# Interleaving the last block's tokens in PSUM, storing them over all 128 partitions, and joining two projection bursts

## The chip, the cores and the metric

One core of one Trainium2 chip runs the whole kernel. The number that counts is the device time of one execution in microseconds (us). Shares of time below are shares of the profiled execution, whose span from first to last instruction is 306.2 us.

The engines are named as in the profile: PE is TensorE (its weight loads are PEld), DVE is VectorE, ACT is ScalarE, POOL is GpSimd, SP is SyncE. A queue that only issues DMAs is written SPq, ACTq or POOLq.

## What is computed

A kernelised attention feeds a two-layer perceptron. Shapes: 8 batches, 8 heads, 576 tokens, head dimension 64, 128 random features; the perceptron takes 4608 tokens of 512 and has 2048 hidden units.

```python
def _attn_ref(q, k, v, omega):
    # q, k scaled by D ** -0.25
    def phi(x):
        h = x @ omega.T - sum(x * x) / 2
        return exp(h - max(h)) / sqrt(m)
    q_p, k_p = phi(q), phi(k)
    kv = einsum('bhsm,bhsd->bhmd', k_p, v);  z = sum(k_p, axis=2)
    return (q_p @ kv) / (q_p @ z + 1e-6)          # [8, 8, 576, 64]

def _moe_ref(x, w_in, w_out):                      # x: [4608, 512], the heads side by side
    h = x @ w_in                                   # [4608, 2048]
    g = h * clip(h + 3, 0, 6) / 6
    return g @ w_out                               # [4608, 512]
```

576 tokens are not a multiple of 128. The kernel takes 512 tokens of each batch as that batch's own block (blocks 0 to 7) and gathers the 64 left over from each of the 8 batches into a ninth block of 512 (block 8). Column `64 * b + s` of that block is left-over token `s` of batch `b`; with `b = 2 * t + a` it is column `(t a s)`, t slowest.

## The kernel before

The program is a list of operations with their dependencies. A table `ORDER` gives each engine its sequence, which was found by a search outside the kernel. PSUM is one ring of eight banks; an operation claims the banks that it needs at its place in PE's sequence and they come free when their last reader is done.

**Projections of queries and keys, batches 3 to 7.** Two 64-row matmuls run side by side in the array's two halves of rows. Each entry of `BURSTS` is one such burst over a range of token columns. The small range `(0, 2)` holds the left-over rows and takes two banks; each of the others takes four.

```python
TU = [(0, 2), (2, 6), (6, 10), (10, 14), (14, 18)]
BURSTS = [[(0, 2)], [(2, 6)], [(6, 10)], [(10, 14)], [(14, 18)]]
...
def burst(n, ranges):
    parts = [(d0, d1, [Virt(ring, True) for _ in range(2 if d1 - d0 == 2 else 4)]) for d0, d1 in ranges]
    ...
    def e(E):
        for part in parts:
            d0, d1, _ = part
            for x in range(d1 - d0):
                for lh in range(2):
                    E.matmul(out_of(part, 0, lh)[0][:, 128 * x:128 * x + 128], kT[64 * lh:64 * lh + 64, d0 + x, :],
                             om[64 * lh:64 * lh + 64, lh, :], start=x == 0, stop=True, skip_group_check=True)   # L766
            for lh in range(2):
                ins = E.matmul(out_of(part, 1, lh)[0], om[64 * lh:64 * lh + 64, lh, :],
                               qT[64 * lh:64 * lh + 64, d0:d1, :], start=d1 - d0 == 4, stop=True,
                               skip_group_check=True)                                                           # L769
        return ins
    # then four exponentials on ACT for each range empty its banks
```

**First layer of blocks 7 and 8.** A seven-product scheme (Strassen's, in Winograd's form) over 2 x 2 blocks. One product is two accumulating matmuls of 256 columns into half a PSUM bank:

```python
def two(E, dst, w, x, start=False):
    for c in range(2):
        ins = E.matmul(dst, w(c), x[:, c, :], start=start and c == 0, stop=c == 1, skip_group_check=True)   # L1126
    return ins

def e_a(E):
    two(E, half(U, 0), orig(0, 0), b[0][0], True)
    return two(E, half(U, 1), summed(W3s), X3s[u])
def e_b(E):
    two(E, half(V, 1), summed(W2s), X2s[u])
    return two(E, half(U, 0), orig(0, 1), b[1][0])
# mm1c: one more two() into half(V, 0)
def e_d(E):
    two(E, half(V, 1), orig(1, 1), X4s[u])
    return two(E, half(V, 0), summed(W4s), b[1][1])
```

These run for `f` = 0 to 7 in each of the two blocks. ACT and DVE move seeds and sums between the halves, apply the activation, and write `gT` (hidden units on partitions, tokens along the row) in the column order that PSUM has.

**Second layer and stores of block 8.** `gT[:, f, 128 * j:128 * j + 128]` is the stationary operand, so 128 consecutive token columns become the 128 output partitions. With columns `(t a s)` partitions 0 to 63 are batch `2t` and 64 to 127 are batch `2t + 1`, so each store is cut into two of 64 partitions.

```python
def last_product():
    for n, (j, e0, e1) in enumerate(((0, 0, 256), (1, 0, 128), (1, 128, 256))):
        ...  # eight matmuls (L1371), one DVE addition (L1379), then
        for x in range(2):
            ... E.dma_start(ends[x, MAIN:S, j, 256 + e0:256 + e1], osb[64 * x:64 * x + 64, j, 256 + e0:256 + e1])   # L1383

def store(blk, i, c0, c1, t):
    ...
    else:                                           # block 8
        x = out.rearrange("(t a s) e -> a s t e", a=2, s=S)
        parts = [(64 * a, 64, x[a, MAIN:S, 2 * i:2 * i + 2, c0:c1]) for a in range(2)]
    for p0, n, dst in parts:
        ... E.dma_start(dst, osb[p0:p0 + n, 2 * i:2 * i + 2, c0:c1])                                                # L1400
```

Block 8 has three calls of `store` (six DMAs) and three pieces in `last_product` (six more): twelve DMAs, spread over SPq and ACTq.

Of the kernel before, what the change touches and what calls it, by code (L numbers as in the profile page):

```python
# [20 lines left out]
        118, 13, 124, 139, 144, 156, 115, 150, 168, 147, 153, 133, 127, 121, 142, 162, 165, 183, 171, 159, 175, 177,  # L21
        136, 185, 212, 130, 173, 197, 214, 179, 219, 254, 199, 187, 181, 242, 227, 189, 204, 202, 257, 229, 244, 217,
        222, 403, 404, 232, 234, 415, 247, 416, 417, 409, 410, 249, 411, 405, 406, 412, 418, 207, 421, 424, 252, 237,
        260, 280, 427, 430, 433, 300, 436, 288, 284, 282, 439, 286, 442, 306, 303, 445, 290, 315, 324, 309, 448, 451,
        312, 292, 294, 454, 296, 318, 457, 298, 333, 321, 583, 584, 331, 573, 337, 574, 335, 575, 339, 585, 586, 587,
        327, 341, 588, 576, 353, 345, 589, 343, 577, 329, 355, 366, 578, 579, 593, 368, 379, 371, 594, 595, 358, 392,
        590, 384, 381, 394, 397, 580, 374, 596, 597, 598, 361, 387, 603, 400, 599, 600, 621, 627, 624, 639, 636, 604,
        630, 642, 645, 505, 651, 492, 660, 501, 654, 495, 657, 486, 605, 507, 511, 606, 503, 607, 474, 509, 666, 483,
        498, 477, 480, 672, 608, 669, 513, 489, 609, 792, 610, 675, 519, 782, 515, 517, 527, 783, 539, 798, 541, 544,
        532, 551, 785, 529, 786, 563, 793, 556, 565, 568, 553, 695, 795, 796, 702, 799, 801, 802, 723, 805, 806, 709,  # L30
        736, 809, 815, 716, 824, 812, 818, 830, 741, 827, 839, 833, 842, 748, 854, 848, 845, 750, 860, 738, 760, 857,
        772, 753, 863, 765, 970, 774, 777, 971, 762, 980, 973, 974, 981, 883, 986, 983, 984, 890, 987, 989, 990, 897,
        1003, 1000, 1012, 997, 993, 994, 1006, 911, 1015, 924, 1021, 1027, 929, 1018, 936, 1033, 1030, 904, 926, 1048,
        1042, 1036, 941, 938, 1045, 960, 1051, 1174, 1158, 1159, 965, 948, 962, 1168, 953, 950, 1161, 1071, 1169,
        1162, 1078, 1171, 1172, 1175, 1085, 1177, 1178, 1191, 1092, 1185, 1188, 1194, 1200, 1215, 1203, 1112, 1206,
        1209, 1218, 1181, 1182, 1124, 1117, 1224, 1221, 1230, 1236, 1114, 1099, 1239, 1233, 1126, 1136, 1346, 1347,
        1129, 1141, 1138, 1356, 1148, 1349, 1150, 1153, 1350, 1357, 1259, 1287, 1359, 1360, 1266, 1362, 1365, 1366,
        1273, 1363, 1379, 1376, 1373, 1382, 1388, 1300, 1394, 1369, 1302, 1312, 1391, 1305, 1314, 1397, 1370, 1317,
        1406, 1336, 1409, 1418, 1338, 1403, 1421, 1412, 1280, 1424, 1427, 1550, 1341, 1534, 1535, 1544, 1454, 1537,
        1545, 1447, 1324, 1538, 1326, 1329, 1547, 1548, 1461, 1551, 1553, 1468, 1557, 1554, 1488, 1475, 1490, 1558,  # L40
        1500, 1493, 1561, 1502, 1505, 1512, 1579, 1517, 1514, 1567, 1582, 1524, 1570, 1526, 1600, 1529, 1591, 1564,
        1615, 1609, 1594, 1576, 1606, 1585, 1612, 1660, 1673, 1597, 1663, 1629, 1665, 1676, 1702, 1630, 1668, 1678,
        1689, 1632, 1633, 1692, 1639, 1694, 1705, 1681, 1718, 1707, 1640, 1697, 1731, 1721, 1642, 1723, 1643, 1734,
        1710, 1747, 1736, 1648, 1649, 1760, 1726, 1750, 1739, 1807, 1645, 1763, 1752, 1646, 1765, 1820, 1755, 1810,
        1652, 1812, 1653, 1836, 1768, 1823, 1776, 1825, 1815, 1777, 1839, 1849, 1828, 1841, 1779, 1852, 1865, 1844,
        1854, 1780, 1878, 1868, 1786, 1857, 1870, 1881, 1787, 1894, 1883, 1792, 1907, 1873, 1886, 1897, 1789, 1899,
        1793, 1790, 1910, 1902, 1939, 1912, 1795, 1796, 1915, 1799, 1800, 1923, 1924, 1933, 1934, 1926, 1927, 1936,
        1937, 1940, 1943, 1944, 1960, 1952, 1956,
    ],
    "SP": [  # L50
        0, 21, 17, 32, 23, 22, 31, 19, 25, 26, 27, 24, 29, 28, 30, 269, 270, 271, 469, 473, 472, 471, 470, 592, 602,
        468, 688, 467, 582, 693, 402, 692, 691, 694, 612, 689, 547, 535, 690, 559, 571, 572, 880, 879, 881, 804, 876,
        756, 744, 808, 768, 780, 882, 877, 781, 878, 992, 1067, 996, 1069, 1068, 1070, 932, 1065, 944, 968, 956, 969,
        1066, 1064, 1255, 1184, 1257, 1256, 1258, 1180, 1120, 1252, 1253, 1144, 1132, 1156, 1157, 1254, 1440, 1443,
        1445, 1446, 1368, 1372, 1444, 1441, 1320, 1442, 1344, 1308, 1332, 1345, 1496, 1520, 1508, 1532, 1556, 1560,
        1533, 1651, 1655, 1798, 1802, 1950, 1948, 1949, 1947, 1962, 1959,
    ],
    "ACT": [
        18, 20, 138, 119, 140, 145, 141, 157, 148, 154, 169, 151, 134, 166, 143, 211, 163, 184, 135, 172, 160, 196,
        176, 178, 241, 174, 186, 213, 225, 226, 180, 243, 182, 203, 190, 218, 188, 233, 407, 413, 419, 422, 425, 281,  # L60
        238, 261, 431, 253, 434, 428, 301, 289, 285, 437, 440, 287, 307, 443, 304, 446, 310, 449, 316, 452, 313, 455,
        325, 319, 297, 299, 295, 352, 334, 322, 336, 340, 332, 458, 342, 328, 338, 354, 378, 377, 330, 367, 344, 380,
        346, 393, 375, 362, 388, 401, 622, 591, 628, 625, 640, 631, 581, 601, 637, 643, 652, 646, 493, 661, 506, 655,
        496, 658, 502, 508, 512, 487, 504, 475, 478, 481, 673, 484, 499, 490, 667, 510, 526, 514, 611, 676, 538, 670,
        516, 520, 528, 518, 540, 550, 784, 561, 562, 787, 564, 696, 698, 700, 708, 705, 707, 703, 731, 726, 729, 701,
        724, 735, 728, 715, 714, 710, 737, 712, 816, 717, 810, 719, 813, 721, 819, 746, 828, 759, 831, 825, 840, 843,
        834, 770, 846, 722, 849, 761, 771, 855, 773, 861, 864, 858, 972, 888, 886, 884, 891, 893, 889, 896, 895, 900,
        975, 1004, 1001, 902, 898, 903, 920, 923, 998, 1013, 1007, 914, 912, 916, 1016, 1022, 1019, 1028, 917, 1034,
        1031, 907, 905, 910, 909, 1043, 1037, 946, 1049, 1052, 947, 1046, 1160, 949, 1076, 1072, 1074, 1163, 1084,
        1083, 1081, 1079, 1077, 1086, 1090, 1088, 1091, 1093, 1192, 1095, 1111, 1186, 1098, 1189, 1201, 1204, 1195,  # L70
        1134, 1123, 1207, 1216, 1210, 1125, 1097, 1225, 1219, 1222, 1231, 1237, 1102, 1100, 1105, 1137, 1234, 1240,
        1104, 1348, 1149, 1351, 1264, 1262, 1265, 1293, 1288, 1292, 1267, 1271, 1260, 1290, 1272, 1269, 1274, 1276,
        1296, 1299, 1380, 1295, 1279, 1374, 1311, 1377, 1383, 1278, 1389, 1395, 1313, 1392, 1334, 1335, 1398, 1407,
        1337, 1410, 1419, 1404, 1422, 1413, 1281, 1283, 1285, 1425, 1286, 1428, 1536, 1459, 1457, 1455, 1460, 1450,
        1448, 1539, 1453, 1452, 1484, 1464, 1462, 1467, 1466, 1487, 1469, 1471, 1473, 1489, 1499, 1476, 1478, 1501,
        1480, 1481, 1474, 1513, 1562, 1523, 1568, 1525, 1580, 1571, 1592, 1565, 1583, 1601, 1595, 1577, 1607, 1586,
        1613, 1661, 1662, 1674, 1598, 1664, 1675, 1610, 1677, 1616, 1631, 1669, 1690, 1671, 1691, 1703, 1693, 1682,
        1706, 1684, 1719, 1698, 1720, 1711, 1700, 1722, 1732, 1733, 1735, 1713, 1727, 1748, 1749, 1740, 1762, 1729,
        1742, 1751, 1764, 1809, 1756, 1758, 1811, 1769, 1822, 1816, 1771, 1824, 1837, 1818, 1840, 1850, 1831, 1829,
        1853, 1845, 1866, 1847, 1867, 1858, 1879, 1869, 1880, 1860, 1882, 1874, 1895, 1887, 1889, 1898, 1876, 1909,  # L80
        1903, 1911, 1905, 1916, 1918, 1928, 1946, 1951, 1955, 1963, 1954, 1958,
    ],
    "DVE": [
        16, 10, 11, 5, 4, 12, 123, 15, 7, 14, 125, 8, 116, 146, 9, 126, 191, 158, 128, 122, 155, 6, 209, 170, 167,
        152, 149, 239, 194, 129, 161, 164, 224, 131, 137, 198, 220, 200, 255, 201, 215, 221, 228, 216, 256, 230, 245,
# [317 lines left out]
def _emit(nc, es, q, k, v, omega, w_in, w_out, out):  # L403
    B, H, S, D = q.shape
# [11 lines left out]
    MAIN = 512  # L416
    TU = [(0, 2), (2, 6), (6, 10), (10, 14), (14, 18)]
    HALVES = [(0, 2), (2, 4)]
    SPLIT = 3
    ROWS = 3  # L420
    BURSTS = [[(0, 2)], [(2, 6)], [(6, 10)], [(10, 14)], [(14, 18)]]
    RP = 2.0
    FAST = 4
    APACE = 0.06
# [80 lines left out]
    op = G.op  # L505
# [987 lines left out]
```

The softmax here doesn't subtract the row's maximum and nothing guards it: scores larger than these inputs give would overflow.

## Time and profile before

| what | before |
|---|---|
| time, median of three runs | 309.49 us (308.87 to 312.65) |
| span of the profiled execution | 306.2 us |
| PE busy | 297.7 us (97%) |
| DVE busy | 245.7 us (80%) |
| POOL busy | 233.7 us (76%) |
| ACT busy | 212.8 us (69%) |
| mean DMA rate | 147 GB/s |

Busy time of an engine is the time in which at least one of its instructions is under way. Matmuls overlap by their pipeline's depth, so the duration of one matmul (273 ns for 256 columns) is longer than the distance from one start to the next; that distance is what a stream of matmuls costs.

The kernel has three stretches: about 21 us in which batch 0 is loaded and PE fills its gaps with matmuls that nobody reads, a long dense stretch, and about 5 us from PE's last matmul to the last store's landing.

### The profile page before, as it was taken

The page shows a single profiled execution, that of the slowest core. Times are in us where ns is not written, and L with a number is a line of the kernel's source. Part 1 is how long each engine was busy: PE and PEld are TensorE (multiplying, and loading weights), DVE is VectorE, ACT ScalarE, POOL GpSimd, SP SyncE. Part 2 cuts the span into 40 slices and gives each one's busy share as a digit, 9 for nine tenths or more (in the row PEclk, how much of TensorE's full clock was granted, in tenths as well). Part 3 has the DMA queues.
Part 4 walks back from the last instruction along what each step waited for, and adds up shares of the span by engine and source line. Part 5 has one row for each costly group of instructions (what it writes and reads, how often), then busy time and mean ns, then how long its engine had stood idle before and what let it go on. Part 6 is the DMA issues. An engine that isn't in the chain of part 4 may idle for free.

```text
span 306.2 us, 7368 instructions
## 1 busy us (share of the span) xinstructions
PE 297.7 (97%) x2798; PEld 210.4 (69%) x2798; DVE 245.7 (80%) x539; ACT 212.8 (69%) x511; POOL 233.7 (76%) x247
## 2 busy tenths in 40 slices
PE   7999999999999999999999999999999999999993
PEld 5668866545785468646856586647764788888883
DVE  3978887779898885798596877896889898999953
ACT  4995997578959972889477758876875876675300
POOL 2775657089894989799989896988845999999950
PEclk9999999999999999999999999999999999999999
DMA  8999999999972999999949984998906000210125
GB/s 224 297 187 187 269 163 153 209 206 181 194 187 35 165 143 182 242 155 208 175 104 124 217 222 112 131 130 215 207 20 190 9 0 3 94 45 3 69 88 120
DMA packets 90147, 44.88 MB, mean 147 GB/s; under 512 B 57984, under 2 KB 87808, under 8 KB 90112
## 3 DMA queue, kind: packets, MB, share of 16 engines
q1 hardware_dynamic: 62368, 30.98, 43.5%
q0 software_dynamic: 26592, 12.46, 34.1%
q10 hardware_dynamic: 1152, 0.98, 1.2%
q8 instruction: 22, 0.36, 0.5%
q14 instruction: 13, 0.11, 0.2%
HBM read 36.73 MB, written 9.44 MB: 151 GB/s over the span
## 4 chain that ended last, share of the span: by engine, by line
PE 79%; POOL 10%; DMA 4%; DVE 2%; issue 1%; SPq 1%; ACT 1%; POOLq 0%
PE p L1305 28%; PE p L1047 25%; PE p L1126 5%; PE p L1217 4%; POOL gT L1233 3%; PE p L1192 3%; PE p L978 3%; DMA wi<-in_moe_w_in_dram 3%; POOL s L1233 3%; PE p L950 2%; PE p L766 2%; PE p L769 2%; DMA q<-in_q_dram 1%; SPq L621 1%; PE p L830 1%
## 5 line engine op out<-in xcount | busy, mean ns | idle before, releaser
L1047 PE MATMUL p<-xT,wi 128*128 128x512 f16 x384 | 90.3, 379 | 0.0
L1055 DVE SCALAR_TENSOR_TENSOR gT<-tsb,p 128x512 f16<-128x512 f16 x96 | 62.8, 679 | 12.4 <-ACT tsb L1053 11.6
L1053 ACT ACTIVATE tsb<-p 128x512 f16<-128x512 f32 x96 | 55.4, 600 | 16.5 <-PE p L1047 12.3
L1047 PEld LDWEIGHTS p<-xT,wi 128*128 128x128 f16 x384 | 35.4, 98 | 38.0 <-issue 1.1
L1305 PE MATMUL p<-wo,gT 128*128 128x256 f16 x368 | 45.8, 273 | 0.1
L1233 POOL TENSOR_TENSOR s<-gT 128x512 f16<-128x512 f16 x30 | 34.8, 1161 | 6.8 <-DVE gT L1055 4.8
L1233 POOL TENSOR_TENSOR gT<-gT,s 128x512 f16<-128x512 f16 x31 | 35.8, 1155 | 5.2 <-PE p L1305 3.0
L1233 POOL TENSOR_TENSOR s<-gT,s 128x512 f16<-128x512 f16 x31 | 35.8, 1156 | 4.9 <-DVE gT L1055 2.9
L1305 PEld LDWEIGHTS p<-wo,gT 128*128 128x128 f16 x368 | 35.0, 98 | 6.1 <-issue 0.8
L1233 POOL TENSOR_TENSOR gT<-gT 128x512 f16<-128x512 f16 x31 | 36.1, 1164 | 2.4
L934 POOL TENSOR_TENSOR vc<-v,cc 128x512 bf16<-128x512 f32 x24 | 25.4, 1057 | 12.3 <-DVE cc L928 7.4
L790 DVE TENSOR_REDUCE mx<-kp 128x4 f32<-128x512 bf16 (+1 forms) x50 | 29.9, 619 | 5.0 <-ACT kp L785 5.0
L794 ACT ACTIVATE qpT<-p 128x512 bf16<-128x512 f32 (+1 forms) x50 | 26.9, 564 | 8.6 <-PE p L769 8.6
L785 ACT ACTIVATE kp<-p 128x512 bf16<-128x512 f32 (+1 forms) x50 | 26.2, 559 | 9.3 <-PE p L769 8.6
L1305 PE MATMUL p<-t,gT 128*128 128x256 f16 x256 | 31.4, 273 | 0.0
L994 DVE TENSOR_TENSOR xb<-p,rec 128x256 f16<-128x256 f32 (+1 forms) x64 | 28.8, 471 | 0.6
L621 POOL DMA_DIRECT2D qb<-in_q_dram x28 | 19.5, 705 | 11.5 <-PE p L1047 9.6
L1305 PEld LDWEIGHTS p<-t,gT 128*128 128x128 f16 x256 | 24.3, 98 | 5.1 <-issue 1.2
L522 ACT COPY p<-p 128x256 f32<-128x256 f32 (+1 forms) x46 | 17.7, 398 | 13.2 <-PE p L1126 5.6
L1174 ACT ACTIVATE tsb<-p 128x512 f16<-128x512 f32 x32 | 18.8, 598 | 6.5 <-PE p L1126 3.9
L621 POOL DMA_DIRECT2D kb<-in_k_dram x21 | 16.5, 786 | 7.1 <-PE p L1047 7.1
L1176 DVE SCALAR_TENSOR_TENSOR gT<-tsb,p 128x512 f16<-128x512 f16 x32 | 21.0, 679 | 0.9 <-ACT tsb L1174 0.8
(132 smaller groups left out, 580.4 us busy)
## 6 DMA issues: line engine op xcount, KB each, us to landing
v<-in_v_dram SPq DMA_DIRECT2D x14, 512.0 KB, 4.9
out_dram<-osb SPq DMA_DIRECT2D x14, 512.0 KB, 3.3
kb<-in_k_dram POOLq DMA_DIRECT2D x14, 256.0 KB, 5.4
qb<-in_q_dram POOLq DMA_DIRECT2D x14, 256.0 KB, 5.6
wo<-in_moe_w_out_dram POOLq DMA_DIRECT2D x8, 256.0 KB, 8.2
wi<-in_moe_w_in_dram POOLq DMA_DIRECT2D x3, 512.0 KB, 7.4
q<-in_q_dram SPq DMA_DIRECT2D x4, 256.0 KB, 4.5
vl<-in_v_dram SPq DMA_DIRECT2D x8, 128.0 KB, 4.1
```

The lines of the kernel that those rows point to most:

```text
L621: lambda E: E.dma_start(dst, src), prio + 0.001 * turn_of[0], reads=gate, writes=keys,
L785: op("ACT", actt(128 * (d1 - d0)), lambda E, lh=lh, ko=ko, part=part: E.activation(ko, out_of(part, 0, lh)[0].rearrange("p (x m) -> p x m" ...
L790: op("DVE", dvet(128 * (d1 - d0)), lambda E, ko=ko, mo=mo: E.reduce_max(mo, ko, axis=AX.X), p0 + 0.01, reads=[("kp", 0, d, lh) for d in ra ...
L794: op("ACT", actt(128 * (d1 - d0)), lambda E, lh=lh, part=part: E.activation(qd[:, part[0]:part[1], lh, :], out_of(part, 1, lh)[0].rearrang ...
L934: return E.tensor_tensor(vcm[:, :, 0:D], v32[:, m, :, :], cbc, ALU.mult)
L994: op("DVE", dvet(128 * n), lambda E: E.tensor_tensor(xv(i0, i1), psum()[:, :, :, 0:64], rbc, ALU.mult), t + 0.01, reads=[vn, ("rec", ru)], ...
L1047: ins = E.matmul(ring.t[vh.slot], wi[:, c, 128 * f:128 * f + 128], xv[:, c, :], start=(c == 0), stop=(c == NJ - 1))
L1053: op("ACT", actt(512), lambda E: E.activation(tsb[tu][:], ring.t[vh.slot], AF.Relu, bias=0.5, scale=1.0 / 6.0), t - 0.1, reads=[vh], write ...
L1055: op("DVE", dvet(512), lambda E: E.scalar_tensor_tensor(gT[gu][:, f, :], tsb[tu][:], 1.0, ring.t[vh.slot], ALU.min, ALU.mult), t - 0.1, re ...
L1176: op("DVE", dvet(512), lambda E, v=v, tu=tu, dst=dst: E.scalar_tensor_tensor(dst(), pieces(tsb[tu][:]), 1.0, pieces(v.ring.t[v.slot]), ALU ...
L1233: op(engines, {"POOL": 0.07 + n / 455.0, "DVE": 0.1 + n / 850.0}, lambda E: E.tensor_tensor(dst, x, y, ALU.subtract if minus else ALU.add) ...
L1305: ins = E.matmul(ring.t[v.slot][:, 256 * j:256 * j + 256], a[:, f, 128 * j:128 * j + 128], w[:, f, :], start=(first and f == 0 and j == 0) ...
```

## The change

1. **Interleaved tokens.** For block 8 the outputs of the first layer's matmuls are written to PSUM in column order `(t s a)` instead of `(t a s)`: consecutive columns of the moving operand go to every second fp32 element. From there on, `gT` and everything after it keep that order, and partition `2s + a` of a result is left-over token `s` of batch `2t + a`.
2. **Nine stores.** With the batch pair innermost on the partitions, one DMA over all 128 partitions stores both batches. Three calls of `store` now give two DMAs each (one per `t`), and `last_product` gives three: nine in place of twelve.
3. **One burst for the left-over rows.** The ranges `(0, 2)` and `(2, 6)` become a single burst that claims six banks, so PE goes once instead of twice into its two-row-half form.
4. **A new sequence.** `ORDER` was searched again for the changed program. On PE the last product of the kernel is now the 256-column one; before, it was a 128-column one.

The diff, with the five sequences of `ORDER` cut to one line of each side:

```diff
 ORDER = {
     "PE": [
-        118, 13, 124, 139, 144, 156, 115, 150, 168, 147, 153, 133, 127, 121, 142, 162, 165, 183, 171, 159, 175, 177,
+        13, 118, 124, 150, 139, 168, 115, 156, 144, 121, 153, 147, 133, 162, 127, 165, 177, 183, 159, 130, 185, 136,
         ... (all five engines' sequences are replaced)
@@ -418,7 +418,7 @@
-    BURSTS = [[(0, 2)], [(2, 6)], [(6, 10)], [(10, 14)], [(14, 18)]]
+    BURSTS = [[(0, 2), (2, 6)], [(6, 10)], [(10, 14)], [(14, 18)]]
@@ -1028,6 +1028,9 @@
+    def woven(blk, dst):
+        return dst.rearrange("p (t s a) -> p t a s", s=64, a=2) if blk == 8 else dst
+
@@ -1044,7 +1047,7 @@     (mm1: used by no block 8 here)
-                ins = E.matmul(ring.t[vh.slot], wi[:, c, 128 * f:128 * f + 128], xv[:, c, :], start=(c == 0),
+                ins = E.matmul(woven(blk, ring.t[vh.slot]), wi[:, c, 128 * f:128 * f + 128], xv[:, c, :], start=(c == 0),
@@ -1122,8 +1125,9 @@
         def two(E, dst, w, x, start=False):
+            d = woven(blk, dst)
             for c in range(2):
-                ins = E.matmul(dst, w(c), x[:, c, :], start=start and c == 0, stop=c == 1, skip_group_check=True)
+                ins = E.matmul(d, w(c), x[:, c, :], start=start and c == 0, stop=c == 1, skip_group_check=True)
@@ -1379,27 +1383,27 @@     (last_product)
-            for x in range(2):
-                op(... E.dma_start(
-                    ends[x, MAIN:S, j, 256 + e0:256 + e1], osb[64 * x:64 * x + 64, j, 256 + e0:256 + e1]), ...
+            op(... E.dma_start(
+                ends[:, MAIN:S, j, 256 + e0:256 + e1].rearrange("a s e -> s a e"), osb[:, j, 256 + e0:256 + e1]), ...
     def store(blk, i, c0, c1, t):
         ...
         else:
             x = out.rearrange("(t a s) e -> a s t e", a=2, s=S)
-            parts = [(64 * a, 64, x[a, MAIN:S, 2 * i:2 * i + 2, c0:c1]) for a in range(2)]
+            parts = [(r, 1, x[:, MAIN:S, r, c0:c1].rearrange("a s e -> s a e")) for r in (2 * i, 2 * i + 1)]
         ...
```

## The prediction

> **What bounds the kernel now.** I read the page first. Its parts 1 and 4 say the same thing: PE is busy nearly all the time and is most of the chain that ended last.
>
> ```profile
> PE 297.7 (97%) x2798; PEld 210.4 (69%) x2798; DVE 245.7 (80%) x539; ACT 212.8 (69%) x511; POOL 233.7 (76%) x247
> ...
> PE 79%; POOL 10%; DMA 4%; DVE 2%; issue 1%; SPq 1%; ACT 1%; POOLq 0%
> ```
>
> The POOL share could mislead, so next I cut the span into stretches and read PE's busy time (columns: stretch, its length, then each engine's busy us and instructions, the granted clock, the DMA share, GB/s).
>
> ```profile
> 0.00:21.50 21.50, 18.89 (x202) 13.60 (x202) 14.79 (x48) 15.93 (x42) 13.97 (x24) 1.00 1.04 239
> ...
> 28.70:255.00 226.30, 225.84 (x2097) 150.26 (x2098) 184.46 (x397) 170.33 (x411) 179.19 (x187) 1.00 0.89 156
> 255.00:288.00 33.00, 32.88 (x302) 29.16 (x299) 31.13 (x63) 20.59 (x48) 30.86 (x27) 1.00 0.09 33
> 288.00:301.20 13.20, 13.19 (x128) 11.77 (x128) 9.29 (x16) 1.16 (x2) 6.98 (x6) 1.00 0.31 104
> 301.20:306.20 5.00, 0.19 (x4) 0.02 (x1) 0.50 (x2) 0.00 (x0) 0.00 (x0) 0.85 0.68 147
> ```
>
> From 28.7 to 301.2 us PE lacks 0.59 us of being busy throughout. POOL stands in the chain around 274 to 288 us, but PE has other work there and loses only 0.12 us in 33. So in the middle each us of matmul added or removed is a us of time, and a better sequence has next to nothing to find there. What is not PE is the first 21.5 us (loads: DMA share 1.04) and the 5.0 us at the end.
>
> Now the three parts that the change touches. The chain in order of time gives the price of a first-layer product's matmul (start us, length, what):
>
> ```profile
> 257.31 2.18 PE p L1126 x20
> ```
>
> 20 matmuls of 256 columns in 2.18 us: 109 ns each, start to start. The view of that line counts 48 + 32 + 32 + 32 + 32 + 16 + 16 + 16 = 224 of them in two blocks; the code agrees (14 for each `f`, 8 of `f`): 112 are block 8's, about 12.2 us, from 258.8 us on (first matmul that reads `xS`) to 287.6.
>
> PE's timeline around a burst (start, length, instructions):
>
> ```profile
> 209.77 1.04 PE L1305 MATMUL p<-t,s 128*128 128x256 f16 x8
> 210.74 0.40 PE L766 MATMUL p<-om,kT 64*128 64x128 bf16 x8
> 210.97 0.38 PE L769 MATMUL p<-qT,om 64*128 64x512 bf16 x2
> 211.28 1.05 PE L1305 MATMUL p<-wo,gT 128*128 128x256 f16 x8
> ```
>
> Eight matmuls of 109 ns from 209.77 end their streaming at 210.64; the burst starts at 210.74: 0.10 lost going in. The two 512-column matmuls run side by side, 0.21 from 210.97, so 211.18; the next starts at 211.28: 0.10 lost coming out.
>
> The end: the last piece of the chain, and the view of the line that issues the last stores (issues of each queue with the ns of one, first and last start).
>
> ```profile
> 301.43 0.29 DVE osb L1379
> ```
>
> ```profile
> L1383 ACTq DMA_DIRECT2D out_dram<-osb x4: 502/588/755, 301.4 to 303.5; - x4
> L1383 SPq DMA_DIRECT2D out_dram<-osb x2: 595/600/604, 302.3 to 303.0; - x2
> ...
> DMA to landing us min/median/max: 2.2/2.6/2.9
> ```
>
> The data of the last piece are in SBUF at 301.72, but the last store is issued at 303.5: the queues are still working off earlier issues at about 0.6 us each. 303.5 + 2.6 is 306.1, the end.
>
> **What the Trainium skill says.** *TensorE: Matmul & The Clock Gate*, "Back-to-back issue gap", gives a warm start-to-start distance of N / 2.4 + 2.5 ns: 109.2 for 256 columns. The trace agrees (109). *TensorEngine Tiling (Array Packing)*, "Key Properties": changing the tiling mode drains TensorE; the trace shows 0.10 us each way. *DMA: Bandwidth & Descriptors*, "Rules for kernel authors": two transfers to disjoint partition halves are no gain, use one of 128 partitions; the trace has no such pair to compare, but the queue of issues above is in line with it. *PSUM — Partial Sum Buffer*, "Specifications (TRN2)": PSUM has 8-byte cachelines, and "any non-contiguous AP slows matmuls significantly". No trace here shows it: every PSUM output of the kernel before is contiguous. It is what my prediction turns on.
>
> **The change part by part.**
>
> *Joined burst.* PE visits the two-half form 24 times now: 25 bursts, two of which (181.3 us, 16 matmuls in a row) already follow each other. Afterwards 20. Matmuls are the same. 4 x 0.20 = 0.8 us off PE, in the dense stretch, so off the time. Against it stands the wait for six of eight banks; I set 0 for it and come back below.
>
> *Stores.* Nine DMAs in place of twelve. After the third last addition there are at present eight issues to go through two queues; then five. In the new order the last product is 256 wide, so its addition is 0.42 us instead of 0.29 (both are in the profile for L1379), and it comes after C21's two stores are nearly issued. Counting from the start of PE's last matmul: addition begins 0.3 later, ends at 0.7; the ACT queue is free from C21's store at about 0.9; plus 2.6 to landing and 0.1 to the end is 3.6 us. Before it is 306.2 - 301.2 = 5.0. Gain 1.4; I take 1.3, since the last store is now 128 KB instead of 32.
>
> *Interleaving.* No instruction is added. The 112 matmuls write 256 fp32 with a step of two elements, 8 bytes. If a matmul writes PSUM a line of 8 bytes at a time, a contiguous output needs 128 lines and the interleaved one 256. Suppose the line rate is what the contiguous stream uses now, 128 lines in 106.7 ns. Then the interleaved matmul takes 213 ns (an estimate, from the page's line size and the trace's 109 ns) and loses about 105 ns. 112 x 105 = 11.8 us, all in stretch 255 to 288 where PE is full. Nothing hides it: the other engines just gain slack, and POOL's sums come no later than now. ACT and DVE read these banks contiguously, so their cost stays.
>
> *Sequence.* The middle has 0.6 us to find, some of which a new order can also lose. In the loading stretch the last query load, which opens the way for `w_in`, is issued two places earlier. I give -0.4 in all.
>
> Sum: 309.5 - 0.8 - 1.3 - 0.4 + 11.8 = 318.8 us, with the interleaving at its estimate.
>
> **Rivals.**
>
> *The step costs nothing.* PE's output stream is one element per column and partition whatever its address, and then 309.5 - 2.5 = 307.0 us (-0.8%). For it: the cost that the program itself books for these matmuls isn't changed by the diff, and a step of two touches nothing but addresses. Against: the PSUM page says plainly that it is slow. I give it one chance in four.
>
> *The step costs half as much, or more than double.* Writes may be buffered (half: +5.9, 312.9 us, +1.1%), or accumulation onto half-filled lines may cost a second access (three times the duration: +24, 331). I hold either for unlikely, a twentieth each.
>
> *Six banks stall PE.* Four exponentials of 0.6 us and four of 0.39 on ACT (L785 and L794, by shape) are 4.0 us in which six banks come free only one by one, and PE has two to work in. For it: a second-layer product keeps one bank for 16 or more matmuls, so the two could fill. Against: PE's sequence can put two banks' worth of products there, 32 matmuls being 3.5 us, and PE now loses nothing at the four-bank bursts. If it stalls 0.4 us each time, 5 x 0.4 = 2 us cancel parts one and two. That makes 309 or 321.
>
> *The end does not shorten*, because C21's two 128 KB stores delay the last one on the 16 DMA engines: +0.7.
>
> **Range and chances.** Two humps: about 307 (weight 0.25) and about 318.8 (weight 0.70, a spread of 1.5), with a little between and above. The middle of this mixture is near 318.2. A tenth lies below 306.6, a tenth above 321. 2% is 6.2 us: slower by over 2% means over 315.7, which the second hump clears; the first is within 2%; faster by 2% would need 303.3, which would take twice the gain that I can find.
>
> **What would show it.** Right: the L1126 matmuls that read `xS` start about 213 ns apart while those of block 7 stay at 109; the stretch from the first `xS` matmul to the last product grows by nearly 12 us with POOL idler; 20 visits to L766; the last issue within 0.3 us of the last L1379 addition. The duration of a matmul in the profile is modelled, so I would look at distances between starts, not at durations. Wrong: the distances stay at 109 ns, or PE shows waits before L766 of more than a few tenths, or a wait for POOL appears where PE was full.

## The result and the profile after

The changed kernel takes 317.64 us (median of six runs, 317.15 to 317.9) against 309.13 us for the kernel before (six runs). The ratio is 1.0256, with a 95% interval of 1.0209 to 1.0303: slower by over 2%. The span of the profiled execution grew from 306.2 to 315.5 us.

The page of the changed kernel: the same two lines as before (busy time by engine; the chain's shares).

```profile
PE 307.8 (98%) x2796; PEld 216.5 (69%) x2796; DVE 247.8 (79%) x541; ACT 209.3 (66%) x501; POOL 234.3 (74%) x251
...
PE 83%; POOL 7%; DMA 7%; issue 1%; SPq 1%; ACT 1%; DVE 1%; POOLq 0%
```

PE is busy 10.1 us longer with two matmuls fewer in the trace's count (some records can be missing). So it isn't more work, and over the whole span PE doesn't wait more (8.5 us not busy before, 7.7 now): the same matmuls take longer. By stretch:

```profile
28.70:255.00 226.30, 224.54 (x2097) 150.59 (x2095) 185.33 (x398) 165.73 (x398) 183.30 (x194) 1.00 0.89 155
255.00:297.00 42.00, 42.00 (x286) 31.99 (x284) 27.93 (x56) 21.07 (x47) 30.27 (x27) 1.00 0.07 26
```

From 28.7 to 255 us both kernels do the same number of matmuls, 2097; PE's idle time in that stretch rose from 0.46 to 1.76 us. After it, 33 us before held 302 matmuls, and 42 us now hold 286, with PE busy throughout. The view of the first-layer line splits its matmuls by what they read (the columns are count, then shortest/median/longest ns). The line is L1130 now.

```profile
L1130 PE MATMUL p<-xT,wi x32: 272/273/273, 239.9 to 259.4; 128*128 128x256 f16 x32
...
L1130 PE MATMUL p<-xS,wi x32: 379/421/421, 258.0 to 293.8; 128*128 128x256 f16 x32
...
L1130 PE MATMUL p<-xS,q x16: 421/421/421, 266.7 to 298.5; 128*128 128x256 f16 x16
```

`xT` is block 7, still written contiguously; `xS` is the left-over block, written to every second element. `q` is a buffer that holds sums of weights. Before, all these rows read 272 or 273:

```profile
L1126 PE MATMUL p<-xS,wi x32: 272/273/273, 258.9 to 283.9; 128*128 128x256 f16 x32
```

The chain in order of time gives the distances between starts:

```profile
277.71 3.02 PE p L1130 x14
280.73 0.87 PE p L1309 x8
```

14 matmuls in 3.02 us are 216 ns each. The second-layer matmuls beside them, of the same 256 columns, are at 109. The end of the kernel became shorter (last piece of the chain, and the line that issues the last stores):

```profile
312.11 0.42 DVE osb L1383
```

```profile
L1386 ACTq DMA_DIRECT2D out_dram<-osb x2: 587/682/776, 310.9 to 312.6; - x2
...
DMA to landing us min/median/max: 2.3/2.4/2.6
```

The last store is issued at 312.6, right when its data are ready (312.53), and the span ends at 315.5. Before, the last addition began 4.8 us before the end; now 3.4 us, although it is a longer addition.

### The profile page after: what moved, and what is told of

Read it like the earlier page. It is cut to its first block, busy times and chain, and to the rows that moved or that the text cites. A ratio compares the mean times of both kernels' runs of the same rounds, so it can differ in the third digit from the quotient of the medians.

```text
span 315.5 us, 7375 instructions
## 1 busy us (share of the span) xinstructions
PE 307.8 (98%) x2796; PEld 216.5 (69%) x2796; DVE 247.8 (79%) x541; ACT 209.3 (66%) x501; POOL 234.3 (74%) x251
## 4 chain that ended last, share of the span: by engine, by line
PE 83%; POOL 7%; DMA 7%; issue 1%; SPq 1%; ACT 1%; DVE 1%; POOLq 0%
PE p L1309 29%; PE p L1050 23%; PE p L1130 10%; DMA wi<-in_moe_w_in_dram 5%; PE p L1221 4%; POOL s L1237 3%; PE p L1196 3%; PE p L766 2%; PE p L978 2%; PE p L950 2%; DMA q<-in_q_dram 2%; PE p L769 2%; PE p L830 1%; POOL gT L1237 1%; PE p L810 1%
## 5 line engine op out<-in xcount | busy, mean ns | idle before, releaser
L1050 PE MATMUL p<-xT,wi 128*128 128x512 f16 x384 | 89.1, 379 | 0.0
L1237 POOL TENSOR_TENSOR s<-gT 128x512 f16<-128x512 f16 x31 | 35.8, 1156 | 13.8 <-DVE gT L1180 9.9
L1237 POOL TENSOR_TENSOR gT<-gT,s 128x512 f16<-128x512 f16 x30 | 34.7, 1156 | 8.9 <-PE p L1309 6.7
L1237 POOL TENSOR_TENSOR gT<-gT 128x512 f16<-128x512 f16 x30 | 34.9, 1165 | 2.3
L785 ACT ACTIVATE kp<-p 128x512 bf16<-128x512 f32 (+1 forms) x50 | 26.1, 565 | 10.6 <-PE p L769 10.5
L934 POOL TENSOR_TENSOR vc<-v,cc 128x512 bf16<-128x512 f32 x25 | 26.5, 1059 | 7.9 <-DMA v<-in_v_dram 3.7
L621 POOL DMA_DIRECT2D qb<-in_q_dram x28 | 19.6, 710 | 12.3 <-PE p L1050 11.8
L994 DVE TENSOR_TENSOR xb<-p,rec 128x256 f16<-128x256 f32 (+1 forms) x64 | 28.1, 469 | 0.4
L1325 DVE TENSOR_TENSOR u<-p 128x512 f32<-128x512 f32 x16 | 11.0, 690 | 12.4 <-PE p L1309 12.3
```

Of the source, the lines that this page charges most:

```text
L785: op("ACT", actt(128 * (d1 - d0)), lambda E, lh=lh, ko=ko, part=part: E.activation(ko, out_of(part, 0, lh)[0].rearrange("p (x m) -> p x m" ...
L934: return E.tensor_tensor(vcm[:, :, 0:D], v32[:, m, :, :], cbc, ALU.mult)
L994: op("DVE", dvet(128 * n), lambda E: E.tensor_tensor(xv(i0, i1), psum()[:, :, :, 0:64], rbc, ALU.mult), t + 0.01, reads=[vn, ("rec", ru)], ...
L1050: ins = E.matmul(woven(blk, ring.t[vh.slot]), wi[:, c, 128 * f:128 * f + 128], xv[:, c, :], start=(c == 0), stop=(c == NJ - 1))
L1237: op(engines, {"POOL": 0.07 + n / 455.0, "DVE": 0.1 + n / 850.0}, lambda E: E.tensor_tensor(dst, x, y, ALU.subtract if minus else ALU.add) ...
```

## The experiments

Two theories stood against each other at first. One: each interleaved column costs PE a line of PSUM (8 bytes, by the PSUM page that the prediction quotes) to itself. The other: the new sequence or the six-bank burst cost PE time. All runs below keep the changed kernel's sequence, with single operations put in where a run adds some. Each ratio is to the kernel before as it ran beside that run.

**Contiguous writes, all else kept (e1_plain).** The rows of left-over tokens then come out in another order; no work is left out.

```diff
     def woven(blk, dst):
-        return dst.rearrange("p (t s a) -> p t a s", s=64, a=2) if blk == 8 else dst
+        return dst
```

> The changed kernel with its joined burst, nine stores and new sequence, but the left-over block's matmuls write PSUM contiguously as before (the left-over tokens' rows then come out in another order; no work is left out). Theory (the 8-byte step in PSUM is the cost): the L1130 matmuls of the left-over block go from 216 ns back to 109 ns start to start, 112 x 0.107 = 11.4 us less at the most, time 306.2 us (305.5 to 307.0), and the rest of the change is worth about -2.5 us against the kernel before. Rival (the new sequence or the six-bank burst is what costs): the time stays above 312 us.

Measured: 305.9 us, ratio to the kernel before 0.9862 (0.9787 to 0.9937; the kernel before took 310.14 us here). That is 11.7 us less than the changed kernel. The chain of this run:

```profile
274.66 1.53 PE p L1130 x14
276.19 1.75 PE p L1309 x16
```

14 matmuls take 1.53 us, 109 ns each. The interleaved write alone costs 11.7 us; everything else in the change, taken together, is a gain. The second theory falls as the account of the loss.

**Which property of the write costs (e2_pairs, e3_step4).** Two runs vary the pattern: neighbours kept in pairs with a step after each, and single columns with a step twice as long. In both the rows come out in another order.

```diff
-        return dst.rearrange("p (t s a) -> p t a s", s=64, a=2) if blk == 8 else dst
+        return dst.rearrange("p (h a w) -> p a h w", a=2, w=2) if blk == 8 else dst      # e2_pairs
+        return dst.rearrange("p (s a) -> p a s", a=4) if blk == 8 else dst               # e3_step4
```

> As the changed kernel, but the columns are written in pairs: two neighbours in one 8-byte line, then a step of 16 bytes (the rows come out in another order). Theory (what costs is the number of 8-byte lines touched): every line is filled by neighbours, 109 ns start to start, 306.2 us as with contiguous writes. Rival (any output that is not contiguous is slow): 216 ns, 317.6 us. Between them: about 312.

> As the changed kernel, but single columns are written with a step of four elements (16 bytes) in place of two. Theory (one line for each element, whatever the step): as with a step of two, 216 ns and 317.6 us. Rival (the cost grows with the distance): 300 ns or more and at least 326 us.

Measured: 305.73 us with pairs, 317.97 us with a step of four. The first-layer line's view of each run, pairs first:

```profile
L1130 PE MATMUL p<-xS,wi x32: 272/273/273, 258.1 to 283.1; 128*128 128x256 f16 x32
```

With a step of four:

```profile
L1130 PE MATMUL p<-xS,wi x32: 379/421/421, 257.9 to 293.6; 128*128 128x256 f16 x32
```

Pairs of fp32, 16 bytes from one pair to the next, cost nothing. Single elements cost the same at 8 and at 16 bytes: 421 ns in this view and in the changed kernel's, 317.97 and 317.64 us. So it isn't being non-contiguous that costs, nor the distance: it is whether two columns in succession are neighbours. The pairs here also start on even elements, so that each fills one line of 8 bytes; a pair across two lines was not tried, so that the line itself is the cause is the reading that fits, not one shown apart from neighbourhood. The sentence of the Trainium skill's PSUM page that I quoted ("any non-contiguous AP slows matmuls significantly") is too broad by this measurement; the skill's *Advanced Engine Details and Errata*, "Memory Cachelines", repeats it, but adds what fits this measurement: every two consecutive elements should be contiguous.

**The same interleaving on the read side (e4_read).** PSUM is written contiguously and the moving operand is read in the interleaved order: successive columns alternate between two places 64 fp16 elements (128 bytes) apart. The rows come out as the reference has them.

```diff
-                ins = E.matmul(d, w(c), x[:, c, :], ...)
+                m = x[:, c, :].rearrange("p (t a s) -> p t s a", a=2, s=64) if blk == 8 else x[:, c, :]
+                ins = E.matmul(d, w(c), m, ...)              # d is dst again, as in e1_plain
```

> PSUM is written contiguously and the same interleaving is had by reading the moving operand with a step of 64 elements (128 bytes) in SBUF; the output rows are as the reference has them. Theory (only the write side is bound by lines): 109 ns start to start, 306.2 us, and the change is a gain. Rival (the read side pays as well for jumping): 200 ns or more, 316 us or above.

Measured: 321.04 us, ratio 1.0354 (1.0282 to 1.0426), worse than the write. PE's timeline:

```profile
285.52 1.14 PE L1131 MATMUL p<-xS,wi 128*128 128x256 f16 x4
286.50 0.65 PE L1131 MATMUL p<-x,k 128*128 128x256 f16 x2
286.98 1.04 PE L1310 MATMUL p<-t,s 128*128 128x256 f16 x8
```

Four starts in 0.98 us, then two in 0.48: about 243 ns a matmul. The theory that only the write is bound falls. Two more runs, of one execution each, read in runs of two and of eight elements, which alternate between places 256 bytes apart; their rows come out in another order.

```diff
-                m = x[:, c, :].rearrange("p (t a s) -> p t s a", a=2, s=64) ...
+                m = x[:, c, :].rearrange("p (a g w) -> p g a w", a=2, w=2) ...       # e11_read2; w=8 in e12_read8
```

> Contiguous PSUM writes; the moving operand is read in runs of two fp16 (4 bytes), alternating between two places 256 bytes apart (the rows come out in another order). The read in single elements took 243 ns start to start. Theory (each jump costs, so half the jumps cost half the extra): about 175 ns, 313 us. Rival (two elements[...] are enough for full rate): 109 ns and 306 us.

> As the run before with runs of eight fp16 (16 bytes). Theory (each jump costs): an eighth of the extra, about 126 ns, 307.5 us. Rival (full rate[...]): 109 ns and 306 us.

Measured: 309.81 and 305.83 us. Runs of two elements, in PE's timeline:

```profile
278.48 0.71 PE L1131 MATMUL p<-xS,wi 128*128 128x256 f16 x4
279.02 0.44 PE L1131 MATMUL p<-x,k 128*128 128x256 f16 x2
```

Runs of eight, in the chain:

```profile
268.31 1.97 PE p L1131 x18
```

135 ns with runs of 4 bytes (four starts in 0.54 us), 109 with runs of 16 bytes. Both of my accounts were off for the short run: a cost for each jump would have given 175 ns, and full rate 109. For runs of 16 bytes the rival's 109 is right. Of the 4.0 us between the two times, the matmuls make 112 x 26 ns, 2.9 us; PE also came to the left-over block 1.0 us later in the first of the two traces. Where between 4 and 16 bytes the cost ends was not tried, nor whether the distance (128 bytes for the single elements, 256 for the runs) plays a part.

**Interleaving at another engine (e5_dve2, e10_xcopy).** Both write PSUM contiguously, keep the nine stores and give the reference's rows. In the first, DVE interleaves as it writes `gT`, in two instructions of 256 in place of one of 512 (the diff is shortened):

```diff
-                return E.scalar_tensor_tensor(dst(), pieces(tsb), 1.0, pieces(ring), ALU.min, ALU.mult)
+                for a in range(2):                                        # left-over block
+                    w = bass.AP(gT[gu], 512 * f + 256 * n + a,
+                                [[512 * NF, 128], [512 * 8 + (256 - 512 * n), 2], [128, 2], [2, 64]])
+                    i0, i1 = [x.rearrange("p (k t a s) -> p k t a s", k=2, t=2, a=2)[:, :, :, a, :] for x in (tsb, ring)]
+                    ins = E.scalar_tensor_tensor(w, i0, 1.0, i1, ALU.min, ALU.mult)
```

> PSUM is written contiguously; the interleaving is done where DVE writes gT of the left-over block: each of its 16 products of activation and hidden value is cut into two of 256, each writing every second fp16 element. Stores, burst and sequence are those of the changed kernel, and the rows come out as the reference has them. Theory (interleaving is free for an engine that isn't at PE's write rate; the price is 16 more DVE instructions, about 0.18 us each, 2.9 us, in a stretch of 32 us in which DVE is busy for 28.4): mostly hidden, 306 to 307.5 us, about 1% faster than the kernel before. Rival (DVE becomes the bound there): 309 us or more.

Measured: 305.51 us (304.96 to 306.55, six runs), ratio 0.9892 (0.9867 to 0.9916): faster than the changed kernel and, by about 1%, than the kernel before. DVE's groups by shape, the left-over block's line and then block 7's (after the bar: busy us, mean ns of one):

```profile
L1188 DVE SCALAR_TENSOR_TENSOR gT<-tsb,p 128x256 f16<-128x256 f16 x32 | 12.0, 439 | 1.6 <-ACT tsb L1178 1.6
L1182 DVE SCALAR_TENSOR_TENSOR gT<-tsb,p 128x512 f16<-128x512 f16 x16 | 10.6, 681 | 0.2 <-ACT tsb L1178 0.2
```

Two of 439 ns stand in place of one of 681. That is 0.2 us more by the durations, but successive instructions overlap: by busy time the 16 pairs take 12.0 us where 16 single ones take 10.6, 0.09 us more each and 1.4 in all, half of the 2.9 expected. In the stretch of 32 us where most of them run PE stays busy throughout, with 296 matmuls in both runs, and DVE goes from 28.44 us (e1_plain, first line) to 29.25 (this run):

```profile
255.00:287.00 32.00, 32.00 (x296) 28.67 (x294) 28.44 (x58) 20.44 (x48) 29.90 (x27) 1.00 0.09 34
256.00:288.00 32.00, 32.00 (x296) 28.52 (x294) 29.25 (x72) 20.71 (x48) 29.85 (x27) 1.00 0.09 34
```

The theory holds; the bound that the rival expected isn't reached.

In the second, ACT copies the left-over block's input, interleaved, into a buffer that has come free, and all first-layer matmuls read the copy:

```diff
+        o = op("ACT", actt(512), lambda E, j=j: E.copy(xP[:, j, :].rearrange("p (q s a) -> p q a s", q=4, a=2),
+                                                       xS[:, j, :].rearrange("p (q a s) -> p q a s", q=4, a=2)), ...)   # j = 0..3
```

> PSUM is written contiguously; the interleaving is had by four ACT copies (512 columns each) of the left-over block's input into a free buffer, with a step of two fp16 on the write, spread between ACT's work from 240 to 249 us. Rows as the reference has them. Theory: ACT has slack there (7.5 of 10 us busy), its copies of 0.6 us delay an evacuation here and there: 306 to 307.5 us. Rival (each copy stands in front of an evacuation that PE waits for): 308.3 us, 2.4 us more than with contiguous writes alone.

Measured: 305.84 us, ratio 0.9904 (0.9878 to 0.9931). The copies, in the view of their line:

```profile
L1111 ACT COPY xb<-xS x4: 767/772/782, 240.9 to 248.7; 128x512 f16<-128x512 f16 x4
```

They took 0.77 us each and not 0.6, and PE's list of waits from 238 to 300 us is empty. The theory holds here as well. The two don't differ clearly from each other or from contiguous writes.

**The stores (e8_twelve).** Contiguous PSUM, tokens in the order of before and the twelve stores of before, each second piece right behind the first on the same queue; rows as the reference has them. The diff shows `last_product`; `store` is cut in two in the same way.

```diff
-                ends[:, MAIN:S, j, 256 + e0:256 + e1].rearrange("a s e -> s a e"), osb[:, j, 256 + e0:256 + e1])
+            for x in range(2):
+                ends[x, MAIN:S, j, 256 + e0:256 + e1], osb[64 * x:64 * x + 64, j, 256 + e0:256 + e1])
```

> Contiguous PSUM writes, tokens in the order of before, and the twelve 64-partition stores of before in place of nine; joined burst and new sequence stay. Rows as the reference has them. Theory (the last store waits behind earlier issues): from PE's last matmul to the end 5.0 us again in place of 3.75, time 307.2 us. Rival (the gain at the end comes from the new order of the last products): it stays at 3.75 us and 305.9 us.

Measured: 306.51 us, ratio 0.9924 (0.9897 to 0.9952), 0.6 us above e1_plain. The end of this run (last piece of the chain, then the line of the last stores):

```profile
300.40 0.42 DVE osb L1389
```

```profile
L1393 ACTq DMA_DIRECT2D out_dram<-osb x4: 507/615/632, 299.2 to 301.7; - x4
```

And of e1_plain with nine stores:

```profile
300.04 0.42 DVE osb L1383
```

```profile
L1386 ACTq DMA_DIRECT2D out_dram<-osb x2: 582/633/684, 298.8 to 300.5; - x2
```

The last addition ends at 300.82 and 300.46. With twelve stores the last issue comes at 301.7, 0.9 us after its data; with nine at 300.5, at once. From the addition's start to the span's end it is 4.2 us (span 304.6) against 3.45 (span 303.5). Before, it was 4.8 us, with a shorter addition. So of the 1.3 us from 4.8 to 3.45 the number of issues is worth 0.75 (one trace each). The remainder is there with twelve stores too, so it goes with the new order of the last products and of the queues' stores, which no run separates. Neither theory alone is right.

**The joined burst (e9_apart).** The left-over rows' projections as a burst of their own, one PE operation ahead of the other; contiguous PSUM, rows in another order.

```diff
-            op("PE", SWITCH + 2 * mmt(128 * total), e, p0, ... writes=virts, alloc=virts, ...)      # six banks
+            for part in parts[::-1]:
+                o = op("PE", SWITCH + 2 * mmt(128 * (d1 - d0)), lambda E, part=part: e(E, [part]), p0, ...)
+            G.extra.append((made[1], made[0], -AHEAD_R))                                            # two banks, one place earlier
```

> Contiguous PSUM writes with nine stores (rows in another order), but the left-over rows' projections are again a burst of their own, set one PE operation ahead of the other, so that PE visits the two-half form 25 times and not 20. Theory (0.20 us a visit, six banks cost nothing): the distance from the first L766 to the last grows from 136.8 to 137.8 us. Rival (waiting for six banks costs what the visits save): it grows by 0.3 us at most, and the 0.95 us wait before the burst at 220 us is gone.

Measured: 306.86 us in time, ratio 0.9931 (0.9898 to 0.9964), 1.0 us above e1_plain, which is within the runs' spread. The distance from the first burst to the last is steadier. The lines that start the bursts, of e1_plain:

```profile
L766 PE MATMUL p<-om,kT x180: 216/216/227, 84.2 to 221.4; 64*128 64x128 bf16 x180
```

and of this run:

```profile
L773 PE MATMUL p<-om,kT x180: 215/216/228, 83.8 to 222.1; 64*128 64x128 bf16 x180
```

137.2 us from the first to the last matmul of the line became 138.3: 1.1 more. Nine of the ten traces with the joined burst have 137.2 or 137.3 us here; one, e11_read2, has 138.8, so a single trace can be off by as much. PE made 24 visits, not 25: in one batch the separate burst landed right behind another. The wait that I had seen in the changed kernel (in its list of PE's waits, columns total, times, longest)

```profile
PE p L766 <- DVE osb L1325: 0.8, 1, 0.8
```

stays, a little shorter, when the burst there takes only four banks:

```profile
221.94 0.40 PE L773 MATMUL p<-om,kT 64*128 64x128 bf16 x8 [0.59 <-ACT qpT L805]
```

So joining the bursts saves about 1 us by this one trace, and of the wait of 0.8 us only 0.2 goes away with four banks in place of six. 4 visits at 0.20 us are 0.8 of the 1.1; this run doesn't show where the other 0.3 is.

## Why the prediction was right

The predicted time was 318.2 us with 306.6 to 321.0 as its range; measured were 317.64 us. The chance of slower by over 2% had been put at 0.70 (with one in four and two twentieths for the rivals the weights add up to 1.05). That 318.2 comes so close is partly luck: it is the middle of two cases, and the case that came true stood at 318.8, 1.2 us too slow. Of that 0.4 is the kernel before, 309.13 us and not 309.49; most of the rest lies in the small parts.

- *Interleaving, +11.8 us.* Measured by undoing it alone: 317.64 - 305.9 = 11.7. The estimate of 213 ns a matmul met 216. The line rate behind it was a supposition, and this measurement bears it out. The pair and step-of-four runs fit the reason given, lines, and not just the number; they leave open only whether a pair must lie within one line. The section of the Trainium skill that gave 109.2 ns (*TensorE: Matmul & The Clock Gate*, "Back-to-back issue gap") calls its formula that of an isolated matmul, which at large N counts too much for a stream with weight loads; here, with a weight load to each matmul, the stream keeps to it at 256 columns, with 109 ns.
- *PE has no slack to hide it.* Right: PE is busy 42.00 of 42 us there, and the next, its weight loads and POOL, 32.0 and 30.3.
- *Joined burst, -0.8 us.* Measured 1.1 by undoing it, in one trace. A wait of more than a few tenths before L766 was named as a sign of being wrong, and one came, of 0.8 us, once. As 0.6 of it is there with four banks too, the rival, a stall for six banks at every joined burst, did not come true.
- *Stores, -1.3 us.* The size was right, 4.8 to 3.4 us from the last addition to the end (1.4) with a longer addition. Of its causes the count of issues is 0.75 us; the prediction named the last product's new place as well, but gave no share to either.
- *Sequence, -0.4 us.* Not resolved. By the medians, 309.13 to 305.9 us is 3.2 for all but the interleaving, where I had 2.5; less 1.1 and 1.3, about 0.8 is left. By the two profiled executions (spans of 306.2 and 303.5 us) it is 2.7, and 0.3 is left. In the dense stretch the changed kernel waits 1.3 us more than before: PE's idle time from 28.7 to 255 us was 0.46 us and is 1.76 (1.71 in e1_plain). What the sequence gains must lie elsewhere. The loading stretch varies between runs of one sequence: PE's wait for `w_in` is 1.3 us in e5_dve2 and 1.1 us or less in the others.

```profile
PE p L1205 <- DMA wi<-in_moe_w_in_dram: 1.3, 1, 1.3
```

- *What would show it.* I had warned that durations of matmuls are modelled and wouldn't show it. They did: 421 in place of 273 ns. But they overstate it: 148 ns more where the starts are 107 apart. The distances remain the reading that adds up: from the first matmul that reads `xS` to the last of its line, 28.7 us became 40.5, the 11.8 predicted.

The rivals on the step itself (no cost, half the cost, more than double) are refuted by 216 ns against e1_plain's 109.

## What to carry to other kernels

On a stretch where PE is full, an access pattern that looks free is priced by its start-to-start distance: here the write to PSUM was at full rate when every two columns in succession were neighbours, and the moving operand when read in runs of 16 bytes. A reordering that halves the rate of PE is better put on an engine with slack: on DVE's write it cost 0.09 us a product, and no time that the runs can tell from contiguous writes. At the end of a kernel, count the DMA issues behind the last result: each of them took 0.5 to 0.9 us of its queue here.

## What was not expected

The read side of a matmul pays too, and for the same number of elements it paid more than the write: single fp16 columns from alternating places took 243 ns for 256 columns, pairs 135, runs of eight 109; the write took 216 for single fp32 and 109 for pairs. For pieces of 4 bytes it is the other way, 135 for the read and 216 for the write. And the weight loads of interleaved-write matmuls read 139 ns in place of 98 (the view of the first-layer line), although their own operand hadn't changed; in the scattered-read run they stay at 97 to 98:

```profile
L1130 PEld LDWEIGHTS p<-xS,wi x32: 97/139/139, 257.9 to 293.5; 128*128 128x128 f16 x32
```

```profile
L1131 PEld LDWEIGHTS p<-xS,wi x32: 97/98/98, 258.3 to 296.7; 128*128 128x128 f16 x32
```

What lengthens the recorded weight load was not tried.
